# Transposing q and k by DMA instead of TensorE, with v loaded from ScalarE's queue, in a top-k attention and Fourier-mix kernel

## The chip, the cores and the metric

The kernel runs on one core of a Trainium2 chip. The metric is the device time in microseconds (us), the median of three executions. Beside it stands one execution taken by the hardware profiler, from which all durations come.

## The reference

Attention over 8 batches of 8 heads, 576 tokens, head size 64, in which each query keeps its 32 largest scores; then, on the heads joined to 512 channels, a real two-dimensional Fourier transform, a normalisation and a two-layer MLP (512 to 2048 to 512).

```python
def _attn_ref(q, k, v):                         # (8, 8, 576, 64) each
    scores = scale * np.matmul(q, k.transpose(0, 1, 3, 2))
    kth = np.partition(scores, -top_k, axis=-1)[..., -top_k:-top_k + 1]
    scores = np.where(scores >= kth, scores, -1000000000.0)
    attn = np.exp(scores - np.max(scores, axis=-1, keepdims=True))
    attn = attn / (np.sum(attn, axis=-1, keepdims=True) + 1e-09)
    return np.matmul(attn, v)

def _moe_ref(x, w_ch1, w_ch2):                  # x: (8, 576, 512)
    u = x + np.real(np.fft.fft(np.fft.fft(x, axis=1), axis=2))
    un = (u - mean(u)) / np.sqrt(var(u) + 1e-06)
    return u + np.maximum(un @ w_ch1, 0.0) @ w_ch2
```

## The kernel before

**Work and its order.** Two heads make a *pair*; there are 32 pairs, four to a batch. A pair has 9 *tiles* of up to 128 queries: (query block, head) for four full blocks and two heads, and in the middle one tile that holds the last 64 queries of both heads. The program is written out by one loop over *steps* `i`, one step per tile, 288 in all; `r = i % 9` is the step's place in its pair. Each engine executes its instructions in the order in which this loop emits them, and waits at semaphores where the data or the buffer isn't ready. In step `i`:

- TensorE makes the scores of tile `i + 3` (`scores`: part 0 the first 512 keys of both heads, L401, or L386 for the half tile; part 1 the last 64 keys of both heads in one matmul against `kt`, L371). ScalarE copies them from PSUM into an S tile (L404, L393, L375).
- VectorE finds the 32 largest of each row by four rounds of MAX8 (L425) and three of MATCH_REPLACE8 (L427): the last two rounds of tile `i` between the first two of tile `i + 1`.
- GpSimd makes the row's bounds (`bounds`, L434), ScalarE a mask from them (L448), GpSimd subtracts it (L451), ScalarE takes the exponent (`expo`, L459).
- The attention weights are turned for the product with v. Pairs 4 to 30 but 7 (`by_dma`) do it by DMA: ScalarE splits each f32 word into two planes of 16-bit halves (`plane`, L472, in step tile + 2), SP stores them to DRAM (L485, L488) and issues a DMA transpose into `PT` (`turn`, L506, in step tile + 3). The other pairs transpose on TensorE (`transposes`, L527).
- TensorE multiplies with v (`attend`, L564), in two column chunks per pair; a later step turns the result to tokens (`to_tokens`, L604) and VectorE normalises it (L608).

**The rest of TensorE's time** goes to the Fourier transform and the MLP of earlier batches. They are cut into units that wait in a queue. For each stretch between two batches' arrivals a planner (`level`) sets a level of TensorE time per step such that the queue is just emptied; `fixed_cost` is what a step holds by itself, and `some` fills the room up to the level with units (hp L966, cp L993, cv and cw L1163).

**q, k and v.** `load_nat` loads q or k of a pair from SP into the one buffer `nat_t` (L240, L279 for q, six DMAs; L267, L271 for k, three). `prep` transposes its five 128-row blocks on TensorE (L308) and copies them from PSUM on ScalarE: q scaled by 1/8 into `qT` (L316), k into `kT` (L318) and, the last 64 keys, into `kt` (L322). In step r = 0 `prep("q")` works for the next pair, and k's load follows; in step r = 5 `prep("k")`, and the load of the next q follows. `qT` has two buffers, `kT` one. `load_v` issues four DMAs from SP (L288, L255) in step r = 7 for the next pair; v has two buffers.

**Batch 0** (pairs 0 to 3) has no MLP units. There the weights are also loaded and converted: in each step SP loads a 512 KB chunk (L187) into one of five slots, ScalarE scales and splits it (L192, L208, L211), VectorE shifts (L200) and GpSimd joins (L219, L221); SP's next load waits for the join of the chunk whose slot it takes.

Of the kernel before, what the change touches and what calls it, by code (L numbers as in the profile page):

```python
# [9 lines left out]
F32 = mybir.dt.float32  # L10
I32 = mybir.dt.int32
U32 = mybir.dt.uint32
U16 = mybir.dt.uint16
# [6 lines left out]
P = 128  # L20
# [53 lines left out]
def kernel(  # L74
# [73 lines left out]

    kt_t = const.tile([P, P], F32, name="kt", tag="kt")

# [108 lines left out]
    def load_nat(n, pair):  # L259
        if pair < NPAIR:  # L260
            nat[n, pair] = nat_t
            src = q if n == "q" else k
            b, hp = divmod(pair, NPB)
            both = src[b, 2 * hp:2 * hp + 2]
            if n == "k":
                for e in range(2):
                    nc.sync.dma_start(  # L267
                        out=nat_t[:, 0:NF, e, :],
                        in_=both[e, 0:NF * P].rearrange("(c p) d -> p c d", p=P),
                    )  # L270
                nc.sync.dma_start(  # L271
                    out=nat_t[0:TAIL, NF, :, :], in_=both[:, NF * P:S].rearrange("e r d -> r e d")
                )
                return
            for e in range(2):
                for h in range(2):
                    load_half(nat_t, src, pair, e, h)
            for h in range(2):
                nc.sync.dma_start(  # L279
                    out=nat_t[TH * h:TH * (h + 1), NF, :, :],  # L280
                    in_=both[:, HS * h + 2 * P:HS * (h + 1)].rearrange("e r d -> r e d"),
                )

    def load_v(pair):
        if pair < NPAIR:
            v_of[pair] = v_t[pair % 2]
            for e in range(2):
                nc.sync.dma_start(  # L288
                    out=v_of[pair][:, 0:NF, e, :],
                    in_=head_of(v, pair, e)[0:NF * P].rearrange("(c p) d -> p c d", p=P),  # L290
                )
            load_tails(v_of[pair], v, pair)

    def prep(n, pair, blocks=((0, NF), (NF, NC))):

        if pair >= NPAIR:
            return 0.0
        src, got_of = nat[n, pair], qT_of if n == "q" else kT_of
        if pair not in got_of:
            got_of[pair] = attp.tile(  # L300
                [P, S if n == "q" else NF * P], F32, name=f"{n}T_{pair}", tag=f"{n}T",
                bufs=2 if n == "q" else 1
            )
        t_sb = got_of[pair]
        for c0, c1 in blocks:
            tp = ps_t.tile([P, 4, P], F32, name=f"tp{n}_{pair}_{c0}", tag="tp")
            for c in range(c0, c1):
                nc.tensor.transpose(  # L308
                    tp[:, c - c0, :], src[:, c, :, :].rearrange("p h d -> p (h d)"), ident
                )  # L310
            if c0 < NF:
                dst, got = t_sb[:, c0 * P:c1 * P], tp.rearrange("p a c -> p (a c)")[:, 0:(c1 - c0) * P]
            else:
                dst, got = t_sb[:, NF * P:], tp[:, 0, 0:TAIL]
            if n == "q":
                nc.scalar.mul(out=dst, in_=got, mul=scale)  # L316
            elif c0 < NF:
                nc.scalar.copy(out=dst, in_=got)  # L318
            else:
                for e in range(2):  # L320
                    r = slice(D * e, D * (e + 1))
                    nc.scalar.copy(out=kt_t[r, TAIL * e:TAIL * (e + 1)], in_=tp[r, 0, 0:TAIL])  # L322
        return 0.7

# [9 lines left out]
    def scores(i, part):  # L334
# [26 lines left out]
        if part == 1:  # L361

            copy = nc.scalar.copy if i else nc.vector.tensor_copy
            shape, name = [P, NF * P], f"sp_{i}_t"
            if by_dma(i):
                sp = ps_t.tile(shape, F32, name=name, tag="tp")
            else:
                sp = ps_s.tile(shape, F32, name=name, tag="sp") if i else bank(shape, name)

            q_end = P * t + rows  # L370
            nc.tensor.matmul(  # L371
                sp[:, 0:P], lhsT=qT[:, q_end - P:q_end], rhs=kt_t, start=True, stop=True
            )
            for h, (s_t, r, _, tails) in enumerate(to):
                copy(out=s_t[r, tails], in_=sp[P - rows:P, TAIL * h:TAIL * (h + 1)])  # L375
            return 0.3
        if e is None and i >= PER_BATCH:
# [13 lines left out]
            for h, (s_t, r, keys, _) in enumerate(to):  # L391
                for g in range(2):
                    nc.scalar.copy(  # L393
                        out=s_t[r, keys][:, half * g:half * (g + 1)],
                        in_=sps[h][TAIL * g:TAIL * (g + 1), 0:half],
                    )
            return 0.6
        for h, (s_t, r, keys, _) in enumerate(to):
            hd = slice(D * h, D * (h + 1))
            sp = ps_s.tile([P, NF * P], F32, name=f"sp_{i}_{h}", tag="sp")  # L400
            nc.tensor.matmul(  # L401
                sp[r], lhsT=qT[hd, q_cols], rhs=kT[hd, :], start=True, stop=True
            )
            nc.scalar.copy(out=s_t[r, keys], in_=sp[r])  # L404
        return 1.04
# [860 lines left out]
    for t in (kn0, nat_t):  # L1266
        nc.vector.memset(t[TAIL:P, NF, :, :], 0.0)
    nc.vector.memset(kt_t, 0.0)

# [182 lines left out]
    def fixed_cost(i):  # L1452
# [7 lines left out]
        t += 0.0 if ch is None else (CW[ch] / 115.0 + 0.14 * len(CHUNKS[ch]))  # L1460
        if i < N and i % PER_PAIR in (0, 5):
            t += 0.7
        return t + costs.get(i, 0.0)
# [28 lines left out]
    while i < N + 5 or plan or queue or sums:  # L1492
# [12 lines left out]
        e = items[j][2] if j < N else None  # L1505
        preps = []

        q_step = i == 2 if pair_of == 0 else i % PER_PAIR == 0
        if i < N and q_step:
            preps.append(lambda: prep("q", pair_of + 1))  # L1510
        if i < N and i % PER_PAIR == 5:
            preps.append(lambda: prep("k", pair_of + 1))
        if e == 0 and by_dma(j):
            fixed.append(lambda: scores(j, 0) + scores(j, 1))
# [6 lines left out]
        n_mask = 0  # L1521
        fixed += preps

# [27 lines left out]
        if i in arrivals:  # L1551
            carry = min(carry, 0.0) if i > arrivals[0] else -5.0
            run(i, "units")
            step_us = level(i)
        room = step_us - carry - fixed_cost(i)
        cost, got = carry, 0.0
# [8 lines left out]
        for n, fn in enumerate(fixed):  # L1565
# [10 lines left out]

            got += some(max(room * (n + 1) / len(fixed) - got, 1.1 if fn in preps else 0.0))
        if short:
# [14 lines left out]
        if i < N:  # L1593
            if q_step:
                load_nat("k", pair_of + 1)
            if i % PER_PAIR == 5:
                load_nat("q", pair_of + 2)
            if i % PER_PAIR == 7:
                load_v(pair_of + 1)
# [21 lines left out]
        for where in ("pool", "pool2", "load", "load2"):  # L1621
            run(i, where)
        late_now[:] = late_next
        late_next.clear()
# [38 lines left out]
```

## Time and profile before

| | |
|---|---|
| median of 3 executions | 1876.23 us (1875.66 to 1876.60) |
| the profiled execution | 1876.57 us, of which span 1874.8 |
| TensorE matmul busy | 1703.8 us (91%) |
| VectorE busy | 1583.8 us (84%) |
| ScalarE busy | 1295.0 us (69%) |
| GpSimd busy | 912.5 us (49%) |
| DMA queue of SP | 515664 packets, 247.23 MB, 50.9% of 16 engines |
| mean granted TensorE clock | 0.955 |

In the profile PE is TensorE's matmuls and PEld its weight loads, DVE is VectorE, ACT ScalarE, POOL GpSimd, SP the engine that issues most DMAs; a q behind an engine's name (SPq) is its queue. L308 is line 308 of the kernel. A row of the groups reads: line, engine, operation, written tile <- read tiles, shapes, count | busy us, mean ns of one | idle time of the engine before them and what ended it. A matmul of 4-byte data appears as two records where it isn't a transpose. Durations of matmuls overlap, so that a group's count times its mean is more than its busy time. A row of the waits reads: engine, tile and line, what it waited for, then the sum in us, the times, and the longest. A row of the timeline begins with its start and length in us, and neighbours of one kind are merged.

### The profile page before, as it was taken

The numbers are of one execution on the slowest core, as the hardware profiler recorded it, in microseconds if no ns is written. First come the engines' busy times: TensorE is split into PE (matmuls) and PEld (weight loads), VectorE is DVE, ScalarE is ACT, GpSimd is POOL, SyncE is SP. The second block draws the span as 40 slices with busy tenths as digits, with TensorE's granted clock in tenths as the row PEclk, the third lists the DMA queues.
The fourth block names the chain that finished last, engine by engine and source line by source line (L and its number), as shares of the span: only waits on it lengthen the run. The fifth ranks groups of instructions, "written<-read, shape, count | busy, mean of one in ns | idle before, by whom it ended". The sixth has DMA issues, their size and how long they took to land.

```text
span 1874.8 us, 26903 instructions
## 1 busy us (share of the span) xinstructions
PE 1703.8 (91%) x8134; PEld 1086.4 (58%) x8134; DVE 1583.8 (84%) x3301; ACT 1295.0 (69%) x3104; POOL 912.5 (49%) x1278
## 2 busy tenths in 40 slices
PE   5566699789899899999999999989999999999999
PEld 3344465355466555666556565666567555677677
DVE  7999989888899999999999899899999899762110
ACT  6878659577788788877787678767787678652100
POOL 4768643454746266355545465255545364341012
PEclk7777799999999999999999999999999999999999
DMA  5333016661557755586466745694566645530132
GB/s 167 104 98 109 20 46 170 168 164 26 137 146 202 187 130 136 150 209 161 123 161 180 180 114 132 155 231 127 122 162 182 172 121 143 130 111 6 51 114 69
DMA packets 516576, 249.16 MB, mean 133 GB/s; under 512 B 398288, under 2 KB 506448, under 8 KB 516432
## 3 DMA queue, kind: packets, MB, share of 16 engines
q1 hardware_dynamic: 515664, 247.23, 50.9%
q8 instruction: 65, 1.06, 0.2%
q14 instruction: 79, 0.65, 0.1%
q10 hardware_dynamic: 768, 0.21, 0.0%
HBM read 93.63 MB, written 84.74 MB: 95 GB/s over the span
## 4 chain that ended last, share of the span: by engine, by line
PE 55%; DVE 13%; ACT 10%; POOL 10%; issue 6%; DMA 4%; SPq 2%; POOLq 0%; DVEq 0%; ACTq 0%
PE hp L966 22%; PE o L564 7%; DVE wk L427 6%; DVE m L425 6%; PE sp L401 4%; PE cp L993 4%; POOL wk L451 4%; PE cw L1163 3%; PE cv L1163 3%; PE cp L1032 3%; ACT wk L448 2%; POOL fg L651 2%; PE yp L755 2%; ACT wk L472 2%; PE sp_t L371 2%
## 5 line engine op out<-in xcount | busy, mean ns | idle before, releaser
L451 POOL TENSOR_TENSOR wk<-S,wk 128x576 f32<-128x576 f32 x288 | 408.1, 1417 | 549.8 <-ACT wk L448 533.9
L425 DVE MAX8 m<-wk 128x8 f32<-128x576 f32 x864 | 626.5, 749 | 6.2
L966 PE MATMUL hp<-unT,w 128*128 128x256 f32 (+1 forms) x2048 | 529.5, 411 | 5.2 <-ACT unT L884 2.7
L966 PEld LDWEIGHTS hp<-unT,w 128*128 128x128 f32 x2048 | 382.5, 192 | 116.5 <-issue 10.7
L427 DVE MATCH_REPLACE8 wk<-m,wk 128x576 f32<-128x576 f32 x576 | 427.4, 742 | 0.0
L472 ACT COPY wk<-S 128x576 uint16<-128x576 uint16 x468 | 289.1, 668 | 0.0
L448 ACT ACTIVATE wk<-S,nt 128x576 f32<-128x576 f32 x288 | 222.9, 774 | 85.4 <-POOL nt L434 84.5
L564 PE MATMUL o<-PT,v 128*64 128x256 f32 (+3 forms) x1440 | 204.8, 430 | 37.9 <-DMA PT<-planes 19.5
L993 PE MATMUL cp<-w,hT 128*128 128x512 f32 x512 | 236.4, 602 | 0.0
L425 DVE MAX8 m<-S 128x8 f32<-128x576 f32 x288 | 213.5, 741 | 7.8 <-ACT S L375 7.8
L459 ACT ACTIVATE S<-wk,nt 128x576 f32<-128x576 f32 x234 | 184.2, 787 | 48.3 <-POOL wk L451 47.2
L427 DVE MATCH_REPLACE8 wk<-m,S 128x576 f32<-128x576 f32 x288 | 213.5, 741 | 0.0
L970 ACT ACTIVATE hT<-hp 128x320 f32<-128x320 f32 (+1 forms) x256 | 103.9, 412 | 156.3 <-PE hp L966 155.2
L401 PE MATMUL sp<-kT,qT 64*128 64x512 f32 (+1 forms) x528 | 170.7, 676 | 24.2 <-ACT kT L318 9.4
L564 PEld LDWEIGHTS o<-PT,v 128*64 128x64 f32 x1440 | 117.9, 158 | 114.9 <-issue 37.0
L404 ACT COPY S<-sp 128x512 f32<-128x512 f32 (+1 forms) x264 | 141.6, 586 | 24.4 <-PE sp L401 23.3
L993 PEld LDWEIGHTS cp<-w,hT 128*128 128x128 f32 x512 | 93.4, 193 | 91.4 <-issue 91.0
L1108 POOL TENSOR_TENSOR hT<-hT 128x512 f32<-128x512 f32 x64 | 81.6, 1277 | 106.5 <-ACT hT L970 91.5
L434 POOL TENSOR_TENSOR nt<-m,cc 128x2 f32<-128x2 f32 x288 | 59.1, 205 | 126.2 <-DVE m L425 122.5
L371 PEld LDWEIGHTS sp_t<-kt,qT 128*128 128x128 f32 x320 | 51.3, 196 | 108.9 <-issue 70.0
L1163 PE MATMUL cw<-w,hT 128*128 128x256 f32 x448 | 105.0, 381 | 1.5 <-POOL hT L1108 0.9
L527 PE MATMUL tpP<-ident,wk 128*128 128x128 f32 x216 | 40.8, 320 | 61.1 <-ACT wk L459 36.1
(160 smaller groups left out, 2174.3 us busy)
## 6 DMA issues: line engine op xcount, KB each, us to landing
planes<-wk SPq DMA_DIRECT2D x208, 288.0 KB, 2.7
w<-w_parts SPq DMA_DIRECT2D x82, 512.0 KB, 4.7
space<-in_moe_w_ch_dram SPq DMA_DIRECT2D x32, 512.0 KB, 3.7
nat<-in_q_dram SPq DMA_DIRECT2D x128, 64.0 KB, 2.7
v<-in_v_dram SPq DMA_DIRECT2D x64, 128.0 KB, 3.0
out_dram<-x SPq DMA_DIRECT2D x32, 256.0 KB, 2.7
nat<-in_k_dram SPq DMA_DIRECT2D x62, 128.0 KB, 3.0
planes<-wk SPq DMA_DIRECT2D x52, 144.0 KB, 2.6
```

The lines of the kernel that those rows point to most:

```text
L401: nc.tensor.matmul(sp[r], lhsT=qT[hd, q_cols], rhs=kT[hd, :], start=True, stop=True)
L404: nc.scalar.copy(out=s_t[r, keys], in_=sp[r])
L425: ops.append(lambda src=src, m8=m8: nc.vector.max(out=m8, in_=src))
L427: ops.append(lambda src=src, m8=m8: nc.vector.match_replace(w, m8, src, NEG))
L448: nc.scalar.activation(out=w, in_=Ssb[i], func=AF.Relu, scale=-FAR, bias=Nt[i][:, 1:2])
L451: nc.gpsimd.tensor_tensor(out=w, in0=Ssb[i], in1=w, op=ALU.subtract)
L459: nc.scalar.activation(out=Ssb[i] if by_dma(i) else w, in_=w, func=AF.Exp, bias=Nt.pop(i)[:, 0:1], accum_out=den_t[pair % 3][:, c:c + 1],)
L472: nc.scalar.copy(out=words[:, half, :], in_=src[:, half, :])
L564: nc.tensor.matmul(o[D * e:D * (e + 1), c0:c1], lhsT=vv[:, c, e, :], rhs=pt[:, NF if c == NF else (NF + 1) * e + c, c0:c1], start=(c == 0) ...
L966: nc.tensor.matmul(hp[:, 0:w], lhsT=w1[:, dt, P * it:P * (it + 1)], rhs=unT[:, dt, 0:w], start=(dt == 0), stop=(dt == NDT - 1),)
L993: nc.tensor.matmul(cp, lhsT=hT[:, it, P * n:P * (n + 1)], rhs=w2[:, it, :], start=(it == 0), stop=(it == NIT - 1),)
L1163: nc.tensor.matmul(dst, lhsT=h()[a][:, kc, :], rhs=rhs_of(kc), start=start and kc == 0, stop=kc == NK - 1, skip_group_check=True,)
```

## The change

For all pairs but the first, q and k are no longer transposed on TensorE. `split_words` copies the loaded block on GpSimd from `nat_t` into `np_t` as two planes of 16-bit halves, `store_words` writes these to DRAM from SP, and `turn_words` issues two DMA transposes from SP that write `qT` and `kT` as f32 words. `qT` and `kT` have one buffer each. `kT` now holds the last 64 keys of both heads as 128 more columns, each head's other rows zero (`kt` is gone), which is why k's tail is loaded in two DMAs and why GpSimd fills a part of `nat_t` with zeros after q. The scale 1/8 moves from q to the copies of the scores.

The steps are new too: q's load at the end of r = 7 (of the pair before), its split at the end of r = 0, its store and k's load at r = 1, k's split at r = 2, its store at r = 3, the transposes at the end of r = 4 in pairs with DMA-turned attention and of r = 5 in the others. After a pair of the latter kind the first scores of the next pair stand at the end of step r = 6 and not at its start. The planner no longer counts 0.7 us for `prep` in steps 0 and 5. From pair 5 on v is loaded from ScalarE's queue.

```diff
+    np_t = const.tile([P, NC, 2, P], U16, name="np", tag="np")
...
+    def split_words(n, pair):
+        if pair >= NPAIR:
+            return
+        nc.gpsimd.tensor_copy(
+            out=np_t,
+            in_=nat_t.rearrange("p c e d -> p c (e d)").bitcast(U16).rearrange(
+                "p c (x h) -> p c h x", h=2
+            ),
+        )
+        if n == "q":
+            nc.gpsimd.memset(nat_t[0:TAIL, NF, 1, :], 0.0)
+
+    def store_words(n, pair):
+        if pair >= NPAIR:
+            return
+        to = words_of[n, pair] = dramp.tile(
+            [NC * P, 2, P], U16, name=f"{n}w_{pair}", tag=f"{n}w", bufs=2
+        )
+        nc.sync.dma_start(out=to.rearrange("(c p) h x -> p c (h x)", p=P), in_=np_t.rearrange(
+            "p c h x -> p c (h x)"
+        ))
+
+    def turn_words(pair):
+        if pair >= NPAIR:
+            return
+        qw, kw = words_of.pop(("q", pair)), words_of.pop(("k", pair))
+        qT_of[pair], kT_of[pair] = t_qk = (
+            attp.tile([P, S], F32, name=f"qT_{pair}", tag="qT", bufs=1),
+            attp.tile([P, NC * P], F32, name=f"kT_{pair}", tag="kT", bufs=1),
+        )
+        nc.sync.dma_start_transpose(
+            out=t_qk[0].bitcast(U16).rearrange("p (a r) -> p a r", a=1),
+            in_=qw[0:S].rearrange("t h x -> (t h) x"),
+        )
+        nc.sync.dma_start_transpose(
+            out=t_qk[1].bitcast(U16).rearrange("p (a r) -> p a r", a=1),
+            in_=kw.rearrange("t h x -> (t h) x"),
+        )
 
     def load_v(pair):
         if pair < NPAIR:
             v_of[pair] = v_t[pair % 2]
+            queue = nc.sync if pair <= NPB else nc.scalar
...
-            nc.scalar.copy(out=s_t[r, keys], in_=sp[r])
+                sp[r], lhsT=qT[hd, q_cols], rhs=kT[hd, 0:NF * P], start=True, stop=True
+            )
+            nc.scalar.mul(out=s_t[r, keys], in_=sp[r], mul=scale)
...
-        if i < N and i % PER_PAIR in (0, 5):
-            t += 0.7
...
-        if i < N and q_step:
-            preps.append(lambda: prep("q", pair_of + 1))
-        if i < N and i % PER_PAIR == 5:
-            preps.append(lambda: prep("k", pair_of + 1))
-        if e == 0 and by_dma(j):
+        last_scores = []
+        if 0 < j < N and j % PER_PAIR == 0 and not by_dma(j - 1):
+            fixed.append(lambda: 0.0)
+            last_scores = [lambda: scores(j, 0) + (scores(j, 1) if by_dma(j) else 0.0)]
+        elif e == 0 and by_dma(j):
             fixed.append(lambda: scores(j, 0) + scores(j, 1))
...
+        fixed += last_scores
         room = step_us - carry - fixed_cost(i)
...
         for where in ("pool", "pool2", "load", "load2"):
             run(i, where)
+        pair_of, r = divmod(i, PER_PAIR)
+        if r == 7:
+            load_nat("q", pair_of + 2)
+        elif r == 0:
+            split_words("q", pair_of + 1)
+        elif r == 1:
+            store_words("q", pair_of + 1)
+            load_nat("k", pair_of + 1)
+        elif r == 2:
+            split_words("k", pair_of + 1)
+        elif r == 3:
+            store_words("k", pair_of + 1)
+        elif r == (4 if by_dma(i) else 5):
+            turn_words(pair_of + 1)
```

## The prediction

> **What bounds the kernel now.** I read the page first, then sums by stage, the groups by line, the waits of VectorE and TensorE in the middle stage, and the timeline around the places that the change touches. The stages first (columns: busy time and instructions of each engine, TensorE's granted clock, the share of the DMA engines, GB/s):
>
> ```profile
> 0.00:215.00 215.00, 132.30 (x655) 81.73 (x657) 201.60 (x421) 171.44 (x398) 150.43 (x151) 0.78 0.37 107
> 215.00:1640.00 1425.00, 1341.51 (x6414) 835.45 (x6411) 1322.81 (x2749) 1071.30 (x2578) 711.53 (x1055) 0.97 0.58 147
> 1640.00:1875.00 235.00, 230.04 (x1071) 169.27 (x1069) 59.39 (x133) 52.23 (x129) 50.50 (x73) 1.00 0.22 70
> ```
>
> In batch 0 (to 215 us) VectorE sets the pace (201.6 of 215; TensorE 132). From 215 to 1640 both are nearly full: TensorE lacks 83 us, VectorE 102. The tail is TensorE alone and no part of the change lies in it. Whom VectorE waits for in the middle stage, and then whom TensorE waits for (sum, times, longest):
>
> ```profile
> DVE x L608 <- PE tpx L604: 49.0, 20, 6.7
> ```
>
> ```profile
> PE o L564 <- DMA PT<-planes: 19.5, 5, 6.6
> ...
> PE sp L401 <- ACT kT L318: 9.0, 7, 2.5
> ...
> PE tpk L308 <- ACT S L375: 3.6, 1, 3.6
> ```
>
> VectorE's normalising step waits 49 us for a TensorE that runs late; TensorE's own waits are few, the largest for the DMA transposes of the attention weights. Taking the time of nine tiles from one first MAX8 of a pair to the next: 10 of the 27 pairs 4 to 30 keep VectorE 98 to 99% busy (45.8 to 47.9 us each), the other 17 (47 to 70 us) are led by TensorE. Freed TensorE time counts in those, 17/27 = 0.63.
>
> **What is removed.** The transposes of q and k (line 308) and their copies on ScalarE (316, 318, 322):
>
> ```profile
> L308 PE MATMUL tpq<-ident,nat 128*128 128x128 f32 x160 | 25.5, 285 | 4.9 <-DMA nat<-in_q_dram 4.1 <-ACT S L375 0.5
> L308 PE MATMUL tpk<-ident,nat 128*128 128x128 f32 x155 | 24.9, 295 | 4.7 <-ACT S L375 3.6 <-ACT PT L530 1.0
> L318 ACT COPY kT<-tpk 128x512 f32<-128x512 f32 x32 | 18.8, 586 | 4.9 <-PE tpk L308 4.8
> L322 ACT COPY kt<-tpk 64x64 f32<-64x64 f32 x64 | 13.3, 208 | 0.4
> ```
>
> The mean of 285 ns misleads: five of them follow each other through TensorE in 0.55 us. Summed over the middle stage line 308 is 40.0 us of TensorE; with the waits for kT (9.0) and of tpk (3.6) that no longer exist, 52.6. Times 0.63: **-33 us**. In batch 0 the same relief (11.7 us) is worth nothing, since VectorE leads there. The planner gets 0.7 us more room twice in a pair and spreads the MLP units accordingly; their sum is the same. ScalarE loses 18.9 + 15.8 + 11.2 = 45.9 us in the middle stage. The factor 1/8 moves into copies that exist already: a scaled 512-column read of PSUM takes 590 ns (line 316), a plain one 586, so nothing; if it did cost, it would be 4 ns on some 20 copies a pair. The zero fill of kT at the start takes the place of kt's.
>
> **What is added on TensorE's path: the landing of the transposes.** Both come at the end of step 4 of a pair on SP, behind that step's plane store, and the first scores of the next pair stand at the start of step 6. The kind of transfer is in the profile: a 288 KB transpose is the cheapest in this row (issue lowest/median, then landing):
>
> ```profile
> L506 SPq DMA_TRANSPOSE PT<-planes x130: 1294/2483/7487, 255.6 to 1636.5; - x130
> ...
> DMA to landing us min/median/max: 3.2/4.6/9.5
> ```
>
> So q (288 KB) holds SP for 1.3 us, k (320 KB) for 1.45, and k lands 2.0 us (3.2 - 1.3) after its issue: 4.8 us, with other transfers in the same queue 5.5. TensorE arrives 0.6 us earlier than before, because k's transposes stood in step 5: needed are 6.1 us. What there is, in pair 23:
>
> ```profile
> 1228.34 0.56 SPq L485 DMA_DIRECT2D planes<-wk  x1
> ...
> 1231.34 0.38 SPq L909 DMA_DIRECT2D w<-w_parts  x1
> ...
> 1235.45 1.13 PE L401 MATMUL sp<-kT,qT 64*128 64x512 f32 x4
> ```
>
> From the end of the store (1228.90) to the scores 6.6 us, of which the weight load ahead in the queue takes 2.8: 2.3 us short. Read so for all 26 pairs with DMA-turned attention, the room left is 2.8 to 9.6 us, median 6.8, and the shortfalls against 6.1 add up to 15 us (pair 6: 3.3, 23: 2.3, 8: 2.2, 13: 2.1, 26: 1.9, 18: 1.3, then 19, 27, 5 and 12 with 0.6 to 0.1; sixteen have none). The S copies on ScalarE stand in line behind those scores, so I count it in full: **+15** (between 0, if the landing takes 4.8 and TensorE gets no earlier than now, and 62, if these transposes cost twice the row).
>
> A rule speaks against this: the Trainium skill (VectorE: DVE Perf Modes, The three transpose paths) gives 390 ns for a 128x128 bf16 transpose on TensorE and 1309 on the DMA crossbar, and its rules advise TensorE where PSUM will do. Nineteen blocks at that price one after another would be 25 us a pair, and the sum some 500 us higher. The row above moves 18 such blocks in 2.48 us of issue (576 KB, the median), so the sum goes by the row.
>
> **Batch 0: a new wait.** There the transposes come at the end of step 5 behind a weight load that waits for GpSimd, and the scores now stand at the end of step 6. Pair 1 (the SP line merges this step's load, which ends at 100.8, with the next step's):
>
> ```profile
> 99.42 1.13 PE L401 MATMUL sp<-kT,qT 64*128 64x512 f32 x4
> ...
> 100.43 6.48 SPq L187 DMA_DIRECT2D space<-in_moe_w_ch_dram  x2
> ...
> 103.01 0.78 ACT L448 ACTIVATE wk<-S,nt 128x576 f32<-128x576 f32 x1
> ...
> 105.78 1.04 DVE L200 TENSOR_SCALAR w<-w 128x512 int32<-128x512 int32 x1
> ```
>
> SP is free at 100.8; k lands at 100.8 + 4.8 = 105.6 at the earliest. The scores follow, then two S copies on ScalarE (0.59 each) to 107.5. Queued behind those copies on ScalarE are the mask (line 448, until now at 103.0) and the weight conversion (192, 0.66), so the conversion ends at 109 and VectorE's shift (line 200, until now 105.78) waits 3.2 us. Pairs 0 and 2 read the same (SP free at 49.6 and 155.1). Pair 3 has no weight load there. 3 x 3.2 = 10, and 2 for GpSimd being fuller: **+12** (0 to 16).
>
> **GpSimd.** Two copies of 128 x 1280 16-bit words and a 0.15 us fill per pair. No such copy is in the trace. Lower bound a fill of 513 columns at 521 ns: 1.3 us; upper bound a two-input subtract, 1024 columns at 2368 ns: 3.0. I take 2.2, between a fill and a two-input operation: 62 x 2.2 = 136 us on an engine busy 912 of 1875. The copy for q ends before the next mask needs GpSimd (the mask's ScalarE half comes 2 to 9 us later at that step). The one for k stands 0.9 to 5 us ahead of a subtract (line 451) and delays it by 21 us in all, nearly all in pairs where ScalarE has caught up and waits anyway: **+3** (0 to 30).
>
> The Trainium skill (GPSIMD Engine Reference, Elementwise — side-by-side cycle accounting) has 769 ns for 512 elements of a tight one-input loop; scaled, an estimate of 1.9 us. The term would stay at 2 to 3.
>
> **ScalarE and v.** From pair 5 on ScalarE issues four v loads at the end of step 7. Its three k issues at the start took 0.51 to 0.56 us: 27 x 4 x 0.55 = 59 us, against 45.9 removed. Queued behind them are step 8's mask, exponent and hT copies; no wait comes with them, since v's buffer was last read in step 3. ScalarE is 75% busy and is not the bound, but TensorE waits for its hT copies: **+8** (-10, half of TensorE's 19.5 us of waits for PT, whose plane copies follow ScalarE's relief in step 5, to +25, 0.9 us a pair).
>
> **SP.** Per pair it loses 2.3 us (v) and gains two stores of 0.56, a fourth k load (0.6) and the transposes (2.8). q's load moves past step 6's plane store to step 7, k's from step 0 to step 1. There, store and load of 2.8 us stand between the plane store of tile 8 and its transpose, which waited 2.0 us for the store anyway: it comes 0.8 us later, and TensorE has 0.7 to 8.6 us (median 2.9) left: **+3** (0 to 18).
>
> **Sum:** -33 + 15 + 12 + 3 + 8 + 3 = +8 on the profiled execution (1876.57; span 1874.8 and 1.8 around it), whose time is 0.3 above the median 1876.23: **1884 us**.
>
> **Rivals.** (1) *TensorE's relief wins.* For it: 49 us of VectorE's waits hang on TensorE. Against: a third of the pairs is led by VectorE. If landings are hidden (0) and ScalarE's queue costs nothing: -33 + 12 + 3 + 3 = -15, 1861; with all of the 52.6 us, 1842. It decides once shortfalls in step 6 stay under 10 us. (2) *The landing takes TensorE's place.* If the tall q and k sources (1152 rows of 128) cost twice the row, 8.8 us are needed where 6.8 are there: 62 us instead of 15, and 8 more in batch 0: 1939. Against it: byte for byte the row covers the same transfer. (3) *The relief is no relief:* the planner fills the room with MLP units and VectorE leads wherever it matters; gain and shortfalls cancel, 1876. That the change doesn't do what it says is small: 62 of the 64 groups on line 308 surely go.
>
> **How the numbers follow.** Forecast (slower by a little, 1880 to 1900) 0.42; slower by more 0.12; no change 0.12; rival 1 0.34. A measurement of this kernel can tell 0.2% (3.8 us) from no change. The range leaves out 0.08 below (all of the 52.6 us) and 0.12 above (more than half of rival 2): 1852 to 1912. The forecast's own range is 1880 to 1900.
>
> **What would show it.** Right: line 308 down to 10 transposes; TensorE's waits for qT/kT transposes of 1 to 3 us in a few pairs, and VectorE's shift waiting about 3 us three times in batch 0; VectorE's wait for tpx well under 49. A middle stage shorter by over 15 us, or no waits at step 6, would make it wrong towards rival 1. GpSimd copies over 3 us or transposes issued in over 2 us would make it wrong upwards.

## The result, and the profile after

| | before | after |
|---|---|---|
| median of 4 executions | 1875.96 us | 1922.13 us (1918.21 to 1926.74) |
| ratio, 95% interval | | 1.0247 (1.0221 to 1.0272): slower |
| the profiled execution, its span | 1876.57, 1874.8 us | 1918.21, 1916.4 us |

The forecast was 1884 us, range 1852 to 1912. The sign of the likeliest case was right; of the slowdown of 46 us the sum had 8.

The stages of the changed kernel (columns as before the change: busy time and instructions of each engine, granted clock, share of the DMA engines, GB/s). Here and below the middle stage is cut at the first MAX8 of pair 31, so it is pairs 4 to 30. First the middle stage of the kernel before, cut so (the rest then lasts 259.3 us), then the three of the changed kernel:

```profile
214.90:1615.50 1400.60, 1317.11 (x6297) 819.31 (x6294) 1303.11 (x2707) 1054.88 (x2540) 701.79 (x1045) 0.97 0.58 147
```

```profile
0.00:234.40 234.40, 130.60 (x619) 79.72 (x621) 203.47 (x420) 166.77 (x378) 160.30 (x163) 0.74 0.44 120
234.40:1658.60 1424.20, 1292.36 (x6031) 796.49 (x6028) 1306.81 (x2708) 1014.10 (x2405) 767.77 (x1126) 0.97 0.69 169
1658.60:1916.40 257.80, 253.03 (x1179) 183.84 (x1177) 79.12 (x176) 67.79 (x166) 59.72 (x83) 1.00 0.24 76
```

Batch 0 is 19.5 us longer, the pairs 4 to 30 are 23.6 us longer, the rest is 1.5 shorter. In the middle TensorE is busy 24.7 us less than before (1317.1), and yet the stage is longer: it waits 131.8 us there instead of 83.5. VectorE's wait for the late TensorE is still there. With the stage cut so it was 44.6 us before (the 49.0 of the prediction go on to 1640 us); now it is:

```profile
DVE x L654 <- PE tpx L650: 48.6, 16, 7.3
```

TensorE's largest waits in the middle stage of the changed kernel (sum, times, longest). The first is the predicted landing; the third to fifth, 30.7 us, are ScalarE being late, of which the kernel before had about 4:

```profile
PE sp L447 <- DMA kT<-kw: 29.2, 11, 6.5
PE o L610 <- DMA PT<-planes: 24.8, 12, 6.6
PE tpu L927 <- ACT us L879: 11.9, 6, 2.6
PE mp L858 <- ACT us L879: 11.4, 5, 2.9
PE hp L1012 <- ACT hT L1016: 7.4, 6, 1.7
```

The operations that are new, by their source lines (lowest/median/highest ns), and then what is left of line 308 (now 351) among the groups:

```profile
L291 POOL COPY np<-nat x62: 1240/1250/1443, 19.2 to 1623.6; 128x1280 uint16<-128x1280 uint16 x62
...
L318 SPq DMA_TRANSPOSE qT<-qw x31: 1208/1346/2494, 49.3 to 1636.0; - x31
...
L322 SPq DMA_TRANSPOSE kT<-kw x31: 1256/1478/2767, 51.5 to 1637.4; - x31
```

```profile
L351 PE MATMUL tpq<-ident,nat 128*128 128x128 f32 x5 | 1.5, 426 | 4.0 <-DMA nat<-in_q_dram 4.0
L351 PE MATMUL tpk<-ident,kn 128*128 128x128 f32 x5 | 1.3, 426 | 0.2 <-DMA kn<-in_k_dram 0.2
```

So the prices of single operations were not the error: the transposes issue in the predicted 1.3 and 1.5 us, and a split of GpSimd takes 1.25 us, less than the 2.2 taken. The error is in what these operations make others wait for. In batch 0 and on ScalarE (the waits of the whole execution):

```profile
ACT wk L494 <- DMA v<-in_v_dram: 30.1, 12, 4.5
...
ACT wk L494 <- DMA nat<-in_q_dram: 26.9, 7, 5.1
...
DVE w L200 <- ACT w L192: 19.1, 4, 6.5
```

VectorE's shift waits 19.1 us for the weight conversion (5.6, 5.0 and 6.5 behind pairs 0, 1 and 2, and 2.0 once more). Behind pair 1 the chain is this: kT lands, both heads' scores are made together and end 2.1 us later, ScalarE's two copies follow, then the mask and the conversion, for which VectorE waits (from the timelines of the three engines):

```profile
111.72 2.08 PE L447 MATMUL sp<-kT,qT 64*128 64x512 f32 x4 [5.24 <-DMA kT<-kw]
...
113.83 1.08 ACT L450 ACTIVATE S<-sp 128x512 f32<-128x512 f32 x2 [6.82 <-PE sp L447]
114.80 0.78 ACT L494 ACTIVATE wk<-S,nt 128x576 f32<-128x576 f32 x1
115.47 0.66 ACT L192 ACTIVATE w<-space 128x512 f32<-128x512 f32 x1
...
116.15 1.20 DVE L200 TENSOR_SCALAR w<-w 128x512 int32<-128x512 int32 x1 [4.99 <-ACT w L192]
```

Besides, ScalarE's mask waits for loads of v and even of q, which the mask doesn't read. ScalarE's timeline at the end of step 7 of pair 13 shows how that comes about (start, length; ACTq is ScalarE's queue), with SP's beside it:

```profile
762.12 0.38 ACTq L332 DMA_DIRECT2D v<-in_v_dram  x1
...
762.54 0.65 ACTq L332 DMA_DIRECT2D v<-in_v_dram  x1
762.64 0.77 ACT L505 ACTIVATE S<-wk,nt 128x576 f32<-128x576 f32 x1
763.31 0.19 ACT L505 ACTIVATION_READ_ACCUMULATOR S<-wk,nt 128x1 f32 x1
765.09 2.25 ACTq L255 DMA_DIRECT2D v<-in_v_dram  x2
767.44 0.78 ACT L494 ACTIVATE wk<-S,nt 128x576 f32<-128x576 f32 x1 [3.94 <-DMA nat<-in_q_dram]
```

```profile
761.80 0.57 SPq L531 DMA_DIRECT2D planes<-wk  x1
762.41 2.27 SPq L240 DMA_DIRECT2D nat<-in_q_dram  x4
```

The two large loads of v are issued at once. The two small ones (L255) are not: the first of them waits on a semaphore that is raised when SP's plane store of 761.80 lands (765.1), the second on that of one of q's loads (766.8). Neither has a tile in common with the transfer that it waits for; what they share is the semaphore by which their landing is told. ScalarE computes nothing from 763.5 to 767.4. Over the 27 pairs ScalarE stood idle for 0.9 us in sum ahead of the large issues and for 29.7 ahead of the small ones, nearly all of it in ten pairs.

### The profile page after: what moved, and what is told of

It is laid out like the page before. It is cut to its first block, busy times and chain, and to the rows that moved or that the text cites. A ratio compares the mean times of both kernels' runs of the same rounds, so it can differ in the third digit from the quotient of the medians.

```text
span 1916.4 us, 26371 instructions
## 1 busy us (share of the span) xinstructions
PE 1676.0 (87%) x7824; PEld 1060.1 (55%) x7824; DVE 1589.4 (83%) x3301; ACT 1248.7 (65%) x2949; POOL 987.8 (52%) x1371
## 4 chain that ended last, share of the span: by engine, by line
PE 47%; ACT 15%; DMA 11%; POOL 10%; DVE 6%; issue 5%; SPq 5%; ACTq 1%; POOLq 0%; DVEq 0%
PE hp L1012 19%; POOL wk L497 5%; PE cp L1039 4%; PE sp L447 4%; PE o L610 4%; PE cw L1209 3%; PE cv L1209 3%; ACT wk L518 3%; DVE m L471 3%; ACT wk L494 3%; DVE wk L473 3%; PE yp L801 2%; DMA planes<-wk 2%; DMA kT<-kw 2%; DMA w<-w_parts 2%
## 5 line engine op out<-in xcount | busy, mean ns | idle before, releaser
L610 PE MATMUL o<-PT,v 128*64 128x256 f32 (+3 forms) x1440 | 199.6, 422 | 33.6 <-DMA PT<-planes 24.8
L450 ACT ACTIVATE S<-sp 128x512 f32<-128x512 f32 (+1 forms) x264 | 142.8, 590 | 53.8 <-PE sp L447 51.1
L411 PEld LDWEIGHTS sp_t<-kT,qT 128*128 128x128 f32 x320 | 52.6, 201 | 114.2 <-issue 88.0
L1209 PE MATMUL cw<-w,hT 128*128 128x256 f32 x448 | 109.2, 393 | 5.3 <-POOL nt L480 3.8
L447 PEld LDWEIGHTS sp<-kT,qT 64*128 64x128 f32 (+1 forms) x528 | 45.1, 196 | 111.8 <-issue 57.1
```

The source lines that it names most:

```text
L447: nc.tensor.matmul(sp[r], lhsT=qT[hd, q_cols], rhs=kT[hd, 0:NF * P], start=True, stop=True)
L450: nc.scalar.mul(out=s_t[r, keys], in_=sp[r], mul=scale)
L610: nc.tensor.matmul(o[D * e:D * (e + 1), c0:c1], lhsT=vv[:, c, e, :], rhs=pt[:, NF if c == NF else (NF + 1) * e + c, c0:c1], start=(c == 0) ...
L1209: nc.tensor.matmul(dst, lhsT=h()[a][:, kc, :], rhs=rhs_of(kc), start=start and kc == 0, stop=kc == NK - 1, skip_group_check=True,)
```

## The experiments

Theory 1: TensorE's relief is real, and new waits ate it (batch 0, ScalarE behind v, the landing of kT). Its rivals: the relief was never worth anything (2), or GpSimd and the DMA traffic are the price (3). Times are medians; ratios are against runs of the kernel before on the same chip (its medians there were 1877 to 1879), with a 95% interval. To compare two kernels, their ratios are subtracted and multiplied by 1876; such a difference is uncertain by 5 to 7 us, so that one of 2 to 5 us can't be told from nothing.

**No transposes: what the relief is worth.** The calls of `split_words`, `store_words` and `turn_words` are left out, v comes from SP, every pair's scores are made from pair 0's qT and kT, and a new pair's scores stand at the start of their step, as before the change.

```diff
-        qT, kT = qT_of[pair], kT_of[pair]
+        qT, kT = qT_of[0], kT_of[0]
...
-            turn_words(pair_of + 1)
```

> From the changed kernel: nothing of q and k of pairs 1 to 31 is transposed at all, neither on TensorE nor by DMA: no split, no store, no transposing DMA; every pair's scores are computed from pair 0's qT and kT (so the numbers are not the reference's). q, k and v are still loaded, all by SP, and the scores stand where they stood before the change. It is the ceiling of what taking the transposes from TensorE can bring. Theory 1 (the relief is real, new waits ate it): TensorE's work in the middle falls by the 25 us that the change took from it, its waits stay at some 83 us and batch 0 loses its waits for kT: 1843 us (1835 to 1852). Theory 2 (the relief was never worth anything, TensorE only waits longer for VectorE and the planes): 1866 to 1876 us.

1847.31 us, 0.9843 (0.9815 to 0.987): -29.5 us. Its first two stages:

```profile
0.00:211.70 211.70, 128.32 (x617) 78.13 (x619) 199.22 (x420) 167.12 (x378) 150.22 (x151) 0.76 0.39 110
211.70:1592.20 1380.50, 1290.69 (x6033) 792.62 (x6030) 1303.04 (x2707) 1015.73 (x2405) 700.78 (x1045) 0.97 0.59 149
```

TensorE's work in the middle falls by as much as in the changed kernel, and here the stage is shorter by 20.1 us. Theory 2 falls: the relief is worth about 30 us. This is the relief of TensorE and of ScalarE, which no longer copies the transposes, together; no run parts the two.

**Splits and stores, together and apart.** The same kernel with `split_words` and `store_words` as in the change, then with only the one or the other; the calls are put back like this (and so for k), without `turn_words`.

```diff
+            split_words("q", pair_of + 1)      # words_unread, splits_only
...
+            store_words("q", pair_of + 1)      # words_unread, stores_only
```

> As the kernel without any transposes, but GpSimd's splits and the two stores of a pair are made and land in DRAM as in the change; only the transposing DMAs are left out, and all scores still use pair 0's qT and kT (numbers not the reference's). Theory 1: splits of 1.25 us and stores of some 0.7 MB a pair lie beside other work: 0 to 5 us more than without them. Theory 3 (GpSimd's 62 splits, 78 us, and the DMA traffic are the price): at least 15 us more than without them.

> No transposes and no stores; GpSimd makes the two splits of each pair, v on SP, scores from pair 0's qT and kT (numbers not the reference's). Without splits and stores the time was 1847.3 us, with both 1859.4. Theory 3a (GpSimd's 2.5 us a pair delays its masks and the bounds): 1855 to 1860 us, most of the 12. Theory 3b (the stores are the price, the splits lie beside other work): 1847 to 1850 us.

> The complement: the two stores of each pair (0.33 MB each, from a tile that is zero) and no splits, otherwise as the kernel with splits alone (numbers not the reference's). Theory 3a: 1847 to 1850 us. Theory 3b (the stores crowd the queue on which the planes travel): 1855 to 1860 us.

Together 1859.43 us, 0.9903 (0.988 to 0.9926): 11 us more than without, between the two forecasts. Splits alone 1852.72 us, 0.9871 (0.9855 to 0.9888): 5. Stores alone 1850.97 us, 0.986 (0.9842 to 0.9878): 3. Neither 5 nor 3 can be told from nothing; only the 11 of both together can, and how it divides is not shown.

**Transposes that nobody waits for.** The kernel with splits and stores, and now also the change's two transposes per pair, into tiles that the split has done with.

```diff
-        qT_of[pair], kT_of[pair] = t_qk = (
-            attp.tile([P, S], F32, name=f"qT_{pair}", tag="qT", bufs=1),
-            attp.tile([P, NC * P], F32, name=f"kT_{pair}", tag="kT", bufs=1),
+        t_qk = (
+            np_t.rearrange("p c h x -> p (c h x)").bitcast(F32)[:, 0:S],
+            nat_t.rearrange("p c e d -> p (c e d)"),
         )
```

> The kernel in which splits and stores are made and nothing reads them (1859.4 us), and now the two transposing DMAs of each pair as well, at the change's place in SP's queue, but into the tiles that the split has done with, where nobody reads them; the scores use pair 0's qT and kT and stand at the start of their step (numbers not the reference's). So it has all of the change's DMA traffic and SP's issues, and none of its landings on TensorE's path. Theory 1 (the transposes cost by their landing and by the late scores): 1860 to 1867 us, and the wait for the planes' transposes as long as without them. Theory 3 (they cost by crowding SP's queue and the DMA engines, on which the planes of the probabilities travel): 1880 to 1900 us.

1875.75 us, 0.9988 (0.9967 to 1.001): 16 us more than with splits and stores alone, and as slow as the kernel before. Neither theory's number; theory 3 has most of it. With the change's traffic, but without a single landing on TensorE's path, the relief is already gone.

**The transposes alone; SP's time alone; another place.** From the kernel without transposes: `turn_words` alone, reading one tile stored once; six DMAs of 256 bytes in its place; the same transposes at the end of step 8 in place of 4 or 5.

```diff
-        qw, kw = words_of.pop(("q", pair)), words_of.pop(("k", pair))    # turns_only
+        qw = kw = words_of["q", 1]
...
+        for n in range(6):                      # sp_busy, for the two transposes
+            nc.sync.dma_start(out=sink[n:n + 1], in_=np_t[n:n + 1, 0, 0, :])
...
-        elif r == (4 if by_dma(i) else 5):
+        elif r == 8:                            # turns_later
             turn_words(pair_of + 1)
```

> Neither splits nor stores, but the two transposing DMAs of each pair from one stored tile into tiles that nobody reads, at the change's place in SP's queue (numbers not the reference's). Theory A (each transfer adds its own price): the 16 us that the transposes cost on top of splits and stores, 1863 us (1859 to 1868). Theory B (the transposes cost only where the stores have filled the queue already): 1847 to 1853 us.

> The kernel with the transposing DMAs alone (1867.3 us), but in each pair the two transposes are replaced by six DMAs of 256 bytes each at the same place (some 0.45 us of SP's time each, so 2.7 us a pair, as long as the two transposes take to issue) with next to no traffic; numbers not the reference's. If SP's queue is what the transposes cost: 1862 to 1868 us. If it is the traffic on the DMA engines: 1846 to 1850 us, as without any transposes (1847.3).

> The kernel with the transposing DMAs alone, the same two transposes a pair issued three steps later, at the last step of the pair (numbers not the reference's). If the price is that of the traffic wherever it falls: 1864 to 1870 us. If it is a collision with what SP's queue and the planes do at the change's place: 1848 to 1857 us.

Transposes alone: 1867.32 us, 0.9948 (0.9934 to 0.9962), 20 us more than without. SP's time alone: 1850.05 us, 0.9856 (0.9834 to 0.9877), 2 us. The six held SP for 2.1 us a pair on average and the two transposes for 3.4, so this is not quite the same time; still, holding SP explains little of the 20. At the end of step 8: 1859.15 us, 0.9903 (0.9885 to 0.9921), 11 us: about half of the price is there still, and some 8 us depend on where they stand. The packets of the whole execution, without transposes and with them alone:

```profile
DMA packets 517069, 249.10 MB, mean 135 GB/s; under 512 B 398784, under 2 KB 506945, under 8 KB 516929
```

```profile
DMA packets 595101, 268.75 MB, mean 144 GB/s; under 512 B 476176, under 2 KB 584976, under 8 KB 594960
```

77 thousand more packets under 512 bytes. (The stores alone move about as many bytes in larger ones, and cost 3 us, which can't be told from nothing.) The two profiled executions differ by 10 us only, half of what the medians do. In them pairs 9 to 31 differ by at most 1.7 us each, but for three: pair 20 is 3.1 us longer, pair 24 6.0 and pair 28 2.4, the first pairs of batches 5, 6 and 7. Around pair 24, without transposes and then with them (the column before the last is the share of the DMA engines; it sums the packets' times, which can overlap, and so can pass 1):

```profile
1225.00:1234.20 9.20, 9.20 (x44) 7.50 (x42) 9.06 (x19) 7.46 (x17) 8.09 (x10) 1.00 0.97 238
1234.20:1290.70 56.50, 49.50 (x232) 31.40 (x231) 48.98 (x101) 36.11 (x87) 24.84 (x40) 0.94 0.59 155
```

```profile
1226.00:1235.30 9.30, 8.05 (x37) 5.94 (x36) 9.16 (x19) 6.37 (x14) 4.94 (x5) 1.00 1.11 291
1235.30:1297.80 62.50, 54.62 (x248) 34.82 (x248) 49.12 (x101) 38.49 (x92) 28.25 (x45) 0.92 0.65 166
```

In the 9 us ahead of a new batch's first pair the DMA engines were full already (0.97), and with the transposes still fuller (1.11); TensorE, without a gap there before, does 37 matmul records instead of 44 in that time, GpSimd 5 operations instead of 10, and the work left over is done in the next pair, which has 248 instead of 232. The same holds with splits and stores in place: from there to the transposes that nobody waits for the middle stage grows by 21.7 us in the profiled executions, and 21.2 of them lie in pairs 6, 16, 20, 24 and 28 (the last four begin batches 4 to 7). Without transposes the DMA engines are at 0.97 to 1.10 in the 9.2 us ahead of each of these five; of the other pairs from 5 to 30 only pair 11 comes near (0.96), and the rest are at 0.80 or less, pair 12 too (0.56), which begins a batch and gets no longer.

TensorE's waits name a transfer that came late. In the middle stage its cw units wait for loads of their weights (w from w_parts); first without transposes, then with them, then with the six small DMAs in their place:

```profile
PE cw L1209 <- DMA w<-w_parts: 1.2, 2, 0.8
```

```profile
PE cw L1209 <- DMA w<-w_parts: 6.4, 4, 2.4
```

```profile
PE cw L1199 <- DMA w<-w_parts: 0.2, 1, 0.2
```

The four waits of 6.4 us lie just ahead of pairs 16, 20, 24 and 28. (In the changed kernel such waits are 1.5 us in all.) Ahead of pair 24 SP begins to issue three such loads 9.0 us before the pair with the transposes, and 14.4 us before it without. So the price falls where the DMA engines are full and loads of weights stand behind the transposes. What is not shown is whether fullness by itself is the cause: with the transposes at the end of step 8 the share ahead of pair 24 is 1.12 as well, and TensorE does its 44 records there.

**v: who issues it.** The changed kernel with all of v on SP; the kernel before with v on ScalarE; the changed kernel with only the two small loads back on SP.

```diff
-            queue = nc.sync if pair <= NPB else nc.scalar        # v_on_sp
+            queue = nc.sync
...
-            load_tails(v_of[pair], v, pair, queue)               # v_tails_sp
+            load_tails(v_of[pair], v, pair)
...
+            queue = nc.sync if pair <= NPB else nc.scalar        # before_v_act, from the kernel before
```

> The changed kernel with v of all pairs loaded by SP as before the change; all else as in the change. Theory 1: the 72 us in which ScalarE computes nothing while it issues v are on TensorE's path where ScalarE's results come late (23 us of TensorE's waits for the copies of us, 7 us for hT): about 20 us back, 1902 us (1895 to 1910). Theory 4 (the loss is the landing of kT and batch 0 alone, ScalarE has slack): 1918 to 1924 us; SP might even be later with the transposes then, up to 1930.

> The kernel before with one edit: v of pairs 5 to 31 is loaded from ScalarE's queue, as in the change. Theory 1 (four issues of 0.4 to 0.7 us, and waits among them, stop ScalarE for 2.7 us a pair whatever the rest does): 18 us more than before, 1895 us (1889 to 1901). Rival (it costs only together with the words, whose landings the issues wait for): 1876 to 1885 us.

> The changed kernel (1922 us) with the two small loads of v (the last 64 keys of each head) back on SP's queue and the two large ones kept on ScalarE's. In the changed kernel the two large issues waited 0.9 us in sum over 27 pairs and the two small ones 29.7 us. Theory 1a (the waits ahead of the small issues are the price): nearly all of the 18 to 20 us comes back, 1905 us (1901 to 1909). Theory 1b (the issues themselves are the price, half a us each): half comes back, 1912 us (1909 to 1916).

v on SP: 1902.55 us, 1.0138 (1.011 to 1.0166), 20 us back. Put alone into the kernel before: 1888.72 us, 1.005 (1.0034 to 1.0065), +9.4: between the two forecasts, and there ScalarE stood idle for 2.4 us in sum ahead of the small issues, not 29.7. With the small loads on SP: 1899.12 us, 1.0107 (1.0084 to 1.013), all of the 20 us back (the interval allows a little more). ScalarE's waits for DMAs in that kernel are what is left of 57 us:

```profile
ACT wk L494 <- DMA v<-in_v_dram: 4.7, 6, 1.6
...
ACT wk L494 <- DMA nat<-in_q_dram: 0.7, 1, 0.7
```

So about half of the price would be four issues a pair where ScalarE has no time for them, and the other half, by the difference, their waits for SP's transfers. That division is argued from another kernel and not shown: with the two issues that waited moved to SP nothing of the price is left, though the two large issues still stand on ScalarE (their share, some 5 us, is within the uncertainty). The Trainium skill (DMA: Bandwidth & Descriptors, Issuing engines are not separate DMA queues) says that spreading the issue over engines saves only the sequencer's time, since all run on the same 16 DMA engines; here it saved nothing and cost 20 us. The same page (Anatomy of one DMA — SWDGE (gpsimd) path) says that semaphore waits of a DMA are served by the sequencer that issues it; the timeline above shows what that means when it is ScalarE's.

**Batch 0 on TensorE, two ways.** Pairs 1 to 3 go through `prep` on TensorE, k loaded into the free `np_t`. First at the end of step 5, with the new pair's scores still last in step 6; then behind the old pair's last scores, with the new pair's scores first in step 6 again (and v on SP). The first adds the two `prep` at the end of `fixed`, the second behind its first entry, and has the last two lines as well.

```diff
+        if i % PER_PAIR == 5 and pair_of + 1 < NPB:
+            fixed += [lambda n=n: prep(n, pair_of + 1) for n in "qk"]
...
-        if 0 < j < N and j % PER_PAIR == 0 and not by_dma(j - 1):
+        if j < N and j % PER_PAIR == 0 and j >= PER_BATCH and not by_dma(j - 1):
```

> The changed kernel, but pairs 1 to 3 (batch 0) get q and k transposed on TensorE at the end of the step that computes the last scores of the pair ahead; pairs 4 to 31 by words and DMA as in the change, v as in the change. Theory 1: the three waits for kT of 5.2 to 5.8 us in batch 0, and VectorE's 19 us behind them, go; batch 0 is 15 us shorter and all of it reaches the end: 1907 us (1902 to 1912). Theory 5 (batch 0's delay is taken in by later work, since TensorE's own work is what fills the span): 1916 to 1924 us.

> v of all pairs on SP's queue, and pairs 1 to 3 transposed on TensorE, this time where the kernel before had k's transposes: straight behind the last scores of the pair ahead, with the scores of a new pair at the start of their step again; pairs 4 to 31 by words and DMA as in the change. To be held against the changed kernel with v on SP (1902.6 us, batch 0 ends at 234.9 us). Theory 1 (in batch 0 the cost is the order on TensorE and ScalarE: the new pair's scores come last in their step, and ScalarE's weight conversion and VectorE's shift queue behind their copies; what batch 0 loses reaches the end): batch 0 ends at 215 to 221 us, total 1886 us (1881 to 1892). Theory 5 (later work takes it in): 1899 to 1905 us. If batch 0 still ends beyond 230 us, the single buffer of qT and kT is enough by itself to cost it.

The first: 1922.46 us, 1.026 (1.0222 to 1.0298), nothing gained; batch 0 still ends at 232.4 us. By the number that is theory 5; but VectorE's wait shows that this kernel had not removed what it was to remove. The second: 1888.12 us, 1.0051 (1.0031 to 1.0071), 16 us less than with v on SP alone; batch 0 ends at 217.4 us. VectorE's wait for the conversion in batch 0, first and second kernel:

```profile
DVE w L203 <- ACT w L195: 14.6, 7, 4.3
```

```profile
DVE w L203 <- ACT w L195: 3.7, 5, 1.7
```

So the loss in batch 0 doesn't need a DMA: scores that come late in their step, with ScalarE's mask and conversion behind their copies, are enough. And it does reach the end: 16 us here, and 15 from the kernel with the small loads of v on SP to the one below, which adds the same edit to it.

**The best of it.** As the second kernel of batch 0, with the large loads of v on ScalarE's queue and the small ones on SP's.

> The version that the runs so far point to: pairs 1 to 3 transposed on TensorE at the place of before, the two large loads of v on ScalarE's queue and all small ones on SP's, pairs 4 to 31 by words and DMA. From 1899.1 us with v so and the 14.4 us that batch 0 brought: 1885 us (1881 to 1890), still slower than before, because splits, stores and transposes that nobody waits for already give back what TensorE's relief of 30 us brings. A rival, in which the landings are hidden once batch 0 is in order: 1870 to 1877 us, as fast as before.

1881.96 us, 1.0025 (1.0011 to 1.004): 40 us better than the change, still slower than before by 0.25%. It keeps 35.9 us of waits of TensorE for kT in the middle. A version with two buffers for qT and kT, which would hide the landing, was not tried; the transposes that nobody waits for bound what it could bring: about as fast as before.

## Why the prediction was wrong, term by term

| term | on record, us | measured between | us |
|---|---|---|---|
| TensorE's relief | -33 | before, no transposes | -29.5 |
| splits and stores | +3, and part of SP's +3 | no transposes, words unread | +11 |
| transposes as traffic | the rest of SP's +3 | words unread, transposes unread | +16 |
| landing in step 6, pairs 4 to 30 | +15 | transposes unread, batch 0 as before | +12 |
| batch 0 | +12 | batch 0 as before, v on SP | +16 |
| v on ScalarE | +8 (-10 to +25) | v on SP, the change | +20 |
| sum | +8 | | +46 |

The table's sum closes by construction, since each row is the step from one kernel to the next; every row is uncertain by 5 to 7 us, and in another order the steps could come out otherwise.

- **The relief** came out near its term, and nothing of rival 3 (the planner fills the room) is in the runs. Part of that is luck. The 40.0 us of line 308 hold time in which its records overlap those of its neighbours; without transposes TensorE's busy time in the middle stage falls by 26.4 us (1317.1 to 1290.7). With that in place of 40.0 the product is (26.4 + 12.6) x 0.63 = 25, and the stage got 20.1 shorter in the profiled execution, batch 0, where nothing was expected, 3.2. My sign for it, VectorE's wait for tpx falling well under 49 us, was a bad one: in the changed kernel the relief was spent before it got there.
- **The landing** was right in mechanism, and its price came out near, but not for the reason given: 15 was a sum of ten shortfalls of at most 3.3 us, counted in full. TensorE's wait for kT in the middle is 29.2 us in the changed kernel (11 waits, up to 6.5) and 33.4 in the kernel with batch 0 as before, and the price of landing and late scores together is about 12. Waits twice as long as foreseen and a price of less than half of them made up for each other. Here, then, removing a wait brings less than it lasts.
- **Batch 0** had the right chain with a link too short. In the profile of after, behind pair 1, SP is free at 106.1 and kT lands at 111.7 (5.6 us later; 4.8 was said). From there to the end of ScalarE's copies the prediction's chain has 1.9 us, 0.7 of it for the scores; it is 3.2, because the scores alone take 2.1 (behind 5.2 us without work on TensorE their records last 1.1 to 1.2 us each; in the kernel before they lasted 0.6 to 0.7 there). The conversion ends at 116.1. VectorE waits 5.0 us where 3.2 stood, and 5.6 and 6.5 behind pairs 0 and 2.
- **v on ScalarE**: the step that failed is the sentence "no wait comes with them, since v's buffer was last read in step 3". It looked at the tile alone; ScalarE stood idle for 29.7 us ahead of the small loads, by semaphores that they share with SP's transfers. The upper bound (+25) had covered the size, 20; the value taken, 8, had not.
- **SP's +3 is the term that failed most.** It asked whose issue comes later in SP's queue and how long it holds the queue; SP's time alone cost 2 us, which can't be told from nothing. It had no place for what two stores and two transposes a pair, some 0.6 MB for the two of either kind, do where the DMA engines are at 97% and more already, and to the loads of weights that stand behind them there. I read the mean share (0.58) of the stage and not its full stretches. Splits with stores and transposes as traffic are 27 us together where 6 were put down (SP's 3 and GpSimd's 3). In the profiled executions nearly all of the transposes' part lies in the five pairs behind those stretches; how the 11 of splits and stores come about stays open.
- **GpSimd** was bounded on the wrong side (1.25 us a copy, under the lower bound of 1.3), and the copies alone cost 5 us where 3 stood, which can't be told from nothing. The estimate of 1.9 us from the Trainium skill's figure (GPSIMD Engine Reference, Elementwise — side-by-side cycle accounting) was too high as well.
- **Rival 2** (transposes cost twice the row) fell: the median issue takes 1346 and 1478 ns for q's 9 blocks and k's 10, and from issue to landing it is 4.2 and 3.8 us. The rule that was weighed against the row (the Trainium skill, VectorE: DVE Perf Modes, The three transpose paths) would have, at 1309 ns for each block one after another, an estimated 11.8 and 13.1 us; the row was nearer on the price, and the rule's advice to stay on TensorE was right on the outcome.

Range and chances left out a case in which several small positive terms are all too small at once. They were: batch 0, v, and splits with stores and transposes. The last two were costed as time on one engine's queue.

## What to carry to other kernels

Cost a moved or added DMA three times: its issue on the engine that issues it, its landing on who waits for it, and its traffic in the fullest stretch of the DMA engines that it falls into, with the loads that stand behind it there; the mean share of a stage hides that stretch. That the traffic's price falls there is shown here, how it arises only in part. Be wary of issuing DMAs from an engine whose results are needed soon: an issue can stop that engine for a transfer of another queue with which it shares no data. And a relief of the leading engine can be spent by new waits in the same pair, so price the waits at the places where the relief is to count.

## What the runs showed of the hardware

- A DMA's issue on ScalarE waited up to 3.9 us for the landing of SP's transfers into other tiles, by the semaphore that told both their landings: 29.7 us in 27 pairs ahead of the small loads of v, 0.9 us ahead of the large ones.
- GpSimd copies 1280 16-bit elements per partition, read with a stride of two, in 1.25 us, 0.98 ns an element.
- A DMA transpose of 288 KB holds SP for 1.2 to 2.5 us and lands 3.3 to 5.2 us after its issue. Two such a pair, of 608 KB, cost 20 us of 1847 though nobody waited for them, and 11 at another place in the pair; six tiny DMAs in their place cost 2 and two plain stores of about as many bytes 3, and neither can be told from nothing.
